# Warm-up products from a constant, a PSUM bank for each sum of the first step, and attention work moved later in a fused attention and SwiGLU kernel

## The chip, the cores and the metric

The kernel runs on one core of one Trainium2 chip. The metric is the device time of one execution in microseconds (us), and lower is better. Every execution has its own time and its own mean granted TensorE clock (1.000 is full speed). All executions below are of the state that the listing calls fast. A verdict of faster or slower needs 2%, which is 6.6 us; a smaller difference is called "same".

The engines are PE (TensorE, products), PEld (its weight loads), DVE (VectorE), ACT (ScalarE), POOL (GpSimd) and SP (the queue that issues transfers).

## The reference

```python
def phi(x):                                   # x: (4, 4, 1088, 32)
    a = np.einsum('rd,bhsd->bhsr', S1, x)     # r = 8
    b = np.einsum('rd,bhsd->bhsr', S2, x)
    return np.einsum('bhsi,bhsj->bhsij', a, b).reshape(*x.shape[:-1], r * r)
q_p, k_p = phi(q), phi(k)
kv  = np.einsum('bhsf,bhsd->bhfd', k_p, v)
z   = np.sum(k_p, axis=2)
num = np.einsum('bhsf,bhfd->bhsd', q_p, kv)
den = np.einsum('bhsf,bhf->bhs', q_p, z)[..., None] + 1e-06
x   = (num / den).transpose(0, 2, 1, 3).reshape(4352, 128)
g   = x @ w_gate                              # 128 x 1536
out = (g / (1 + np.exp(-g))) * (x @ w_val) @ w_out
```

The weights and the sketches S1 and S2 arrive as float64 words. The kernel narrows them to float32 on the chip.

## The kernel before

The tokens are cut into 12 blocks (three per batch, of 384, 384 and 320 tokens) and the hidden layer into 12 chunks of 128. A *unit* is one chunk of one block: a gate product and a value product, a silu on ScalarE, and a product of the two on VectorE that writes `hj`. Each unit has a *down* product with `w_out`, which adds into one bank per block.

```python
free_banks = ["g0", "g1", "g2", "acc"]        # the ring of PSUM banks
turn = [0]
def bank(tag=None):
    if tag is None:
        tag = free_banks[turn[0] % len(free_banks)]
        turn[0] += 1
    return psum.tile([P, TB], FP32, tag=tag, name="bank")

def unit(i, j, late=False):
    g, u = bank(), bank()
    for o, w in ((g, wg), (u, wv)):
        nc.tensor.matmul(o[:, 0:n], w[:, j, :], xT[:, t0 : t0 + n], start=True, stop=True)
    nc.scalar.activation(sg[:, 0:n], g[:, 0:n], AF.Silu)
    ...
    nc.vector.tensor_tensor(out=hj[:, 0:n], in0=sg[:, 0:n], in1=u[:, 0:n], op=ALU.mult)

def down():
    ...
    if j == 0:
        acc[i] = bank("g0" if i == 1 else "acc")
    nc.tensor.matmul(acc[i][:, 0:n], wo[:, j, :], hidden.pop((i, j))[:, 0:n], ...)
```

At the start nothing can be hidden. The program runs products that nobody reads (`keep_warm`), then batch 0's first attention step as a serial chain. For one batch, `kv` and `z` are summed, turned by a product with the identity (`turn_kv`, result copied to `kvz`), and multiplied with the query features (`totals`). Then VectorE divides (`dT` is the transposed denominator, `xT` the result).

```python
keep_warm(98, 32)
...
srep = bank()                                 # sketches turned; takes g0
...
keep_warm(3)                                  # lands in the next bank of the ring
```

After six early units the first three blocks run in a list of 30 units, z = 0 to 29. Batch 1's attention is a generator that advances one piece at each z in `groups`. A `catch_up` is the product `hj` of an early unit, put off and made by GpSimd.

```python
groups = (11, 13, 15, 17, 21, 24, 27)
for z, (i, j) in enumerate(seq):
    if z == 17:
        free_banks.pop()                      # "acc" leaves the ring: 4 banks, then 3
    unit(i, j)
    ...                                       # weight conversions of this z
    if z in (2, 4, 8, 14, 20, 22):
        catch_up()
    if z >= 17:
        ...; down()
    if z in groups:
        next(att)
while todo:                                   # the rounds
    for _ in range(4):
        if todo:
            down()
    next(att, None)
```

Batches 1 to 3 follow in a steady loop, in which the next batch's attention is threaded between units.

Of the kernel before, what the change touches and what calls it, by code (L numbers as in the profile page):

```python
# [17 lines left out]
def kernel(  # L18
# [70 lines left out]
    def wide(tag):  # L89
        return psum.tile([P, 2, TB], FP32, tag=tag, name=tag)  # L90
# [80 lines left out]
    warm = const.tile([P, TB], mybir.dt.bfloat16, name="warm")  # L171
    nc.vector.memset(warm[:], 1.0)
# [16 lines left out]
    def keep_warm(n, w=TB):  # L189


        ps = bank(free_banks[turn[0] % len(free_banks)])
        for _ in range(n):
            nc.tensor.matmul(
                ps[0:32, 0:w], warm[:, 0:32], warm[:, 0:w], start=True, stop=True
            )
# [128 lines left out]
    def turn_kv(kvz, kvs, t, kzp):  # L325

        for half in range(2):
            nc.tensor.matmul(  # L328
                kzp[F * half : F * half + F, P * t : P * t + P], kvs[:, t, :], ident[:],
                start=True, stop=True,  # L330
            )
        nc.scalar.copy(kvz[:, t, :], kzp[:, P * t : P * t + P])
# [58 lines left out]
    def totals(n, phq, kvz, tag):  # L391

        w = 32 * n
        nd = wide(tag)[:].rearrange("p g (t w) -> p g t w", t=2)
        for t in (1, 0):
            for h in range(H):
                for half in range(2):
                    r = slice(F * half, F * half + F)
                    nc.tensor.matmul(  # L399
                        nd[32 * h : 32 * h + 32, half, t, 0:w],  # L400
                        kvz[r, t, 32 * h : 32 * h + 32],
                        phq[r, h, 0:w],
                        start=True,
                        stop=True,
                    )
        return nd

    def divide(b, x0, n, nd):


        w = 32 * n
        t0 = S * b + 64 * x0
        dT = apool.tile([P, 2 * XS, 32], FP32, tag="dT", name="dT", bufs=2)
        rc = apool.tile([P, 2 * XS], FP32, tag="rc", name="rc", bufs=2)
        rd = apool.tile([P, 2 * XS, 32], FP32, tag="rd", name="rd", bufs=2)
        nc.vector.transpose(  # L416
            out=dT[:, 0 : 2 * n, :].rearrange("p (a x) t -> p a x t", a=2),
            in_=nd[:, :, 1, 0:w].rearrange("p a (x t) -> p a x t", t=32),
        )
        nc.vector.tensor_scalar_add(rc[:, 0 : 2 * n], dT[:, 0 : 2 * n, 0], 1e-6)  # L420
        nc.vector.reciprocal(rc[:, 0 : 2 * n], rc[:, 0 : 2 * n])
        nc.vector.transpose(
            out=rd[:, 0 : 2 * n, :], in_=rc[:, 0 : 2 * n].unsqueeze(2).to_broadcast([P, 2 * n, 32])
        )
        nc.vector.tensor_tensor(
            out=xT[:, t0 : t0 + 2 * w].rearrange("p (x a t) -> p a x t", a=2, t=32),
            in0=nd[:, :, 0, 0:w].rearrange("p a (x t) -> p a x t", t=32),
            in1=rd[:, 0 : 2 * n, :].rearrange("p (a x) t -> p a x t", a=2),
            op=ALU.mult,
        )  # L430
# [12 lines left out]
    def attention(b):  # L443
# [26 lines left out]
        kzp = wide("b")  # L470
        for t in range(2):
            turn_kv(kvz, kvs, t, kzp[:, t, :])
        yield
        tags = "ab"
        for i, (x0, n) in enumerate(steps):
            phq = query_features(n, query_products(x0, n, tags))
            if i + 1 < len(steps):
                turn_q(*steps[i + 1])
            elif b + 1 < B:
                load_q(b + 1)  # L480
            yield
            divide(b, x0, n, totals(n, phq, kvz, tags[0]))
            tags = tags[::-1]
            yield
# [72 lines left out]
    keep_warm(98, 32)  # L557
# [10 lines left out]
    srep = bank()  # L568
# [8 lines left out]
    keep_warm(3)  # L577
# [11 lines left out]
    prods = [key_products(bank(), *c, aside=(c[1] == NC)) for c in fpieces]  # L589
    phk = apool.tile([P, NC, H, R, R], FP32, tag="phk", name="phk")  # L590
    kvp = wide("b")
    kz, kv = kvp[:, 0, 0 : H * F], kvp[:, 1, 0:F]
# [4 lines left out]
    pss = query_products(*steps[0], ("a", (None, None)))  # L597
    qbs = [query_copy(n, *ps) for ps in pss]
# [7 lines left out]
    kvs = apool.tile([P, 2, F], FP32, tag="kvs", name="kvs")  # L606
    kvz = apool.tile([P, 2, P], FP32, tag="kvz", name="kvz", bufs=2)
    nc.scalar.copy(zq[:], kz)
    part("wg", 0)
    part("wv", 0)  # L610
# [3 lines left out]
    zp = bank()  # L614
# [5 lines left out]
    key_values(kv, phk, *fpieces[2])  # L620
    turn_q(*steps[1])
    nc.vector.tensor_copy(kvs[:, 1, :], zp[:, 0:F])
    turn_kv(kvz, kvs, 1, bank())
    nc.vector.tensor_copy(kvs[:, 0, :], kv)
    turn_kv(kvz, kvs, 0, bank())
    part("wg", 0)
    part("wv", 0)
    nd = totals(n, phq, kvz, "a")
    pss = query_products(*steps[1], ("b", (None, None)))
    qbs = [query_copy(steps[1][1], *ps) for ps in pss]  # L630
    keep_warm(3)
# [12 lines left out]
    nd = totals(steps[1][1], phq, kvz, "b")  # L644
# [16 lines left out]
    nd = totals(steps[2][1], phq, kvz, "a")  # L661
# [18 lines left out]
    groups = (11, 13, 15, 17, 21, 24, 27)  # L680
    for z, (i, j) in enumerate(seq):
# [5 lines left out]
        if z in (2, 4, 8, 14, 20, 22):  # L687
            catch_up()
# [11 lines left out]
    while todo:  # L700
        for _ in range(4):
            if todo:
                down()
        next(att, None)
# [48 lines left out]
```

## Time and profile before

| | before |
|---|---|
| time given for it, 3 executions | 328.15, 328.80 and 328.87 us |
| execution that the profile shows | 327.24 us, mean clock 1.000 |
| span, first to last instruction | 325.5 us |
| first ordinary unit (z = 0) | 29.46 us |
| first unit with a down product (z = 17) | 56.23 us |
| first unit of batch 1 | 103.09 us |
| last end on TensorE | 321.03 us |

The bottom four rows are starts and one end on TensorE in the profile. TensorE is the bound in all stretches after the start (busy 96% of the span, and 86% of the chain that ended last), so the distance between two such marks is what a stretch costs.

### The profile page before, as it was taken

How to read it: one execution, taken by the hardware profiler on the slowest of the kernel's cores; microseconds unless marked ns; L12 is line 12 of the kernel's file. 1: busy time of each engine (PE TensorE's matmuls, PEld its weight loads, DVE VectorE, ACT ScalarE, POOL GpSimd, SP SyncE). 2: the span in 40 equal slices, each digit the busy share in tenths (PEclk: the TensorE clock that was granted, in tenths of full speed). 3: DMA queues.
4: the chain of work that ended last, by engine and by line, in shares of the span. 5: the costliest groups of instructions: out<-in, count | busy, mean ns of one | idle time of the engine just before them, and what ended most of it. 6: DMA issues, size and time to landing. Idle time of an engine off the chain costs nothing.

```text
span 325.5 us, 5806 instructions
## 1 busy us (share of the span) xinstructions
PE 312.0 (96%) x2402; PEld 187.8 (58%) x2402; DVE 159.0 (49%) x330; ACT 99.1 (30%) x230; POOL 38.5 (12%) x53
## 2 busy tenths in 40 slices
PE   6979997999999999999999999999999999999994
PEld 5435544655556665555666656555567655555672
DVE  4796889542455632444552552345544322322321
ACT  3457554423112222323232222223232222222220
POOL 2222442740000060000000050000000000000000
PEclk9999999999999999999999999999999999999999
DMA  7443473020113202100030100000010000100101
GB/s 209 135 159 99 129 224 117 0 71 0 27 20 85 81 0 71 24 2 0 15 81 2 22 2 0 13 13 2 0 26 0 13 7 2 25 0 0 24 2 20
DMA packets 25018, 14.01 MB, mean 43 GB/s; under 512 B 18848, under 2 KB 23072, under 8 KB 24992
## 3 DMA queue, kind: packets, MB, share of 16 engines
q1 hardware_dynamic: 24304, 13.56, 16.1%
q8 instruction: 19, 0.31, 0.4%
q10 hardware_dynamic: 688, 0.08, 0.2%
q14 instruction: 7, 0.06, 0.1%
HBM read 11.41 MB, written 2.23 MB: 42 GB/s over the span
## 4 chain that ended last, share of the span: by engine, by line
PE 86%; DVE 7%; DMA 2%; issue 2%; ACT 2%; POOL 0%; SPq 0%; DVEq 0%
PE bank L500 49%; PE bank L528 27%; PE a L399 2%; PE a L351 2%; DMA kld<-in_k_dram 1%; PE b L351 1%; PE a L305 1%; DVE hj L514 1%; DMA raw<-in_moe_w_out_dram 1%; DVE man L228 1%; DVE man L217 1%; PE b L328 1%; PE b L399 1%; DVE exp L224 1%; DVE exp L216 1%
## 5 line engine op out<-in xcount | busy, mean ns | idle before, releaser
L514 DVE TENSOR_TENSOR hj<-sg,bank 128x384 f32<-128x384 f32 (+1 forms) x138 | 72.6, 528 | 124.4 <-PE bank L500 120.5
L506 ACT ACTIVATE sg<-bank 128x384 f32<-128x384 f32 (+1 forms) x144 | 67.6, 472 | 167.0 <-PE bank L500 167.0
L500 PE MATMUL bank<-xT,wg 128*128 128x384 f32 (+1 forms) x288 | 114.3, 478 | 4.1 <-DVE hj L514 1.9
L500 PE MATMUL bank<-xT,wv 128*128 128x384 f32 (+1 forms) x288 | 112.1, 471 | 0.3 <-DVE hj L514 0.2
L528 PE MATMUL bank<-hj,wo 128*128 128x384 f32 (+1 forms) x288 | 108.6, 470 | 0.0
L500 PEld LDWEIGHTS bank<-xT,wv 128*128 128x128 f32 x288 | 54.0, 190 | 35.7 <-DVE hj L514 4.4
L500 PEld LDWEIGHTS bank<-xT,wg 128*128 128x128 f32 x288 | 52.3, 190 | 38.5 <-issue 5.7
L528 PEld LDWEIGHTS bank<-hj,wo 128*128 128x128 f32 x288 | 54.2, 190 | 33.0 <-issue 1.4
L436 POOL TENSOR_TENSOR zs<-phk 128x1024 f32<-128x1024 f32 x3 | 7.1, 2358 | 114.5 <-PE bank L500 113.0
L379 DVE TENSOR_TENSOR phq<-a,qb 128x384 f32<-128x384 f32 (+1 forms) x11 | 5.8, 530 | 8.2 <-ACT qb L365 8.2
L365 ACT COPY qb<-a 128x384 f32<-128x384 f32 (+1 forms) x11 | 5.1, 461 | 15.1 <-PE b L351 7.6
L416 DVE STREAM_TRANSPOSE dT<-a 128x384 f32<-128x384 f32 (+1 forms) x8 | 4.4, 550 | 10.7 <-PE a L399 10.7
L228 DVE SCALAR_TENSOR_TENSOR man<-raw,man 128x384 f32<-128x384 uint32 (+2 forms) x14 | 9.3, 666 | 0.0
L351 PE MATMUL b<-qT,sq 32*64 32x192 f32 (+1 forms) x176 | 9.2, 324 | 0.0
L351 PE MATMUL a<-qT,sq 32*64 32x192 f32 (+1 forms) x176 | 9.2, 324 | 0.0
L221 ACT ACTIVATE exp<-exp,rebias 128x384 int32<-128x384 int32 (+3 forms) x15 | 8.2, 547 | 3.0 <-DVE exp L216 2.4
L365 ACT COPY qb<-b 128x384 f32<-128x384 f32 (+1 forms) x11 | 5.1, 464 | 12.8 <-PE b L351 8.0
L224 DVE SCALAR_TENSOR_TENSOR exp<-raw,exp 128x384 int32<-128x384 int32 (+2 forms) x14 | 8.0, 569 | 0.9 <-ACT exp L221 0.9
L379 DVE TENSOR_TENSOR phq<-b,qb 128x384 f32<-128x384 f32 (+1 forms) x11 | 5.8, 526 | 4.5 <-ACT qb L365 4.5
L351 PEld LDWEIGHTS a<-qT,sq 32*64 32x64 f32 x176 | 5.5, 131 | 3.9 <-issue 3.4
L544 DVE STREAM_TRANSPOSE o<-bank 128x384 f32<-128x384 f32 (+1 forms) x12 | 6.7, 558 | 1.7 <-PE bank L528 1.3
L232 POOL TENSOR_TENSOR wg<-man,exp 128x384 f32<-128x384 f32 (+2 forms) x5 | 4.6, 926 | 23.9 <-DVE man L228 23.9
(88 smaller groups left out, 163.7 us busy)
## 6 DMA issues: line engine op xcount, KB each, us to landing
kld<-in_k_dram SPq DMA_DIRECT2D x4, 544.0 KB, 4.3
vld<-in_v_dram SPq DMA_DIRECT2D x12, 144.0 KB, 5.0
qld<-in_q_dram SPq DMA_DIRECT2D x3, 544.0 KB, 4.0
raw<-in_moe_w_out_dram SPq DMA_DIRECT2D x4, 384.0 KB, 3.2
out_dram<-o SPq DMA_DIRECT2D x32, 48.0 KB, 1.8
raw<-in_moe_w_gate_dram SPq DMA_DIRECT2D x3, 384.0 KB, 3.2
raw<-in_moe_w_val_dram SPq DMA_DIRECT2D x3, 384.0 KB, 3.5
out_dram<-o SPq DMA_DIRECT2D x14, 40.0 KB, 1.7
```

The costliest lines, as they stand in the source:

```text
L221: nc.scalar.activation(e[:], e[:], AF.Relu, bias=rebias[: shape[0], :], scale=8.0)
L224: nc.vector.scalar_tensor_tensor(out=e[:], in0=hi, scalar=-(1 << 31), in1=e[:], op0=ALU.bitwise_and, op1=ALU.bitwise_or,)
L228: nc.vector.scalar_tensor_tensor(out=f, in0=lo, scalar=2.0**-52, in1=f, op0=ALU.mult, op1=ALU.add)
L351: nc.tensor.matmul(parts[g][F * half : F * half + F, t, 0:w], sq[r, t, :, :].rearrange("p i j -> p (i j)"), qT[r, x0 : x0 + n, half, :], s ...
L365: nc.scalar.copy(qb[:, :, 0:w], both[:, :, 1, 0:w])
L379: nc.vector.tensor_tensor(out=phq[:, 2 * pr : 2 * pr + 2, 0:w], in0=both[:, :, 0, 0:w], in1=qb[:, :, 0:w], op=ALU.mult,)
L399: nc.tensor.matmul(nd[32 * h : 32 * h + 32, half, t, 0:w], kvz[r, t, 32 * h : 32 * h + 32], phq[r, h, 0:w], start=True, stop=True,)
L436: add = lambda o, a, b: nc.gpsimd.tensor_tensor(out=o, in0=a, in1=b, op=ALU.add)
L500: nc.tensor.matmul(o[:, 0:n], w[:, j, :], xT[:, t0 : t0 + n], start=True, stop=True)
L506: nc.scalar.activation(sg[:, 0:n], g[:, 0:n], AF.Silu)
L514: nc.vector.tensor_tensor(out=hj[:, 0:n], in0=sg[:, 0:n], in1=u[:, 0:n], op=ALU.mult)
L528: nc.tensor.matmul(acc[i][:, 0:n], wo[:, j, :], hidden.pop((i, j))[:, 0:n], start=(j == 0), stop=(j == NCH - 1),)
```

## The change

Its intent has four parts. The unread products at the start take their operand from a constant of the program, with no memset before them, and there are more of them. Each sum, turned matrix and total of the first step gets its own PSUM bank, so that none waits for a neighbour's reader. In later batches the two turned halves go to one bank with one copy. Batch 1's attention pieces start six units later, and a round has three down products and not four. The diff, cut to its core:

```diff
-    warm = const.tile([P, TB], mybir.dt.bfloat16, name="warm")
-    nc.vector.memset(warm[:], 1.0)
+    warm = nc.const_aps.tensor(1.0, [P, TB], mybir.dt.bfloat16)
...
-    keep_warm(98, 32)
+    keep_warm(125, 32)
...
-    srep = bank()
+    srep = bank("g0")
...
-    keep_warm(3)
+    keep_warm(7)
...
-    kvp = wide("b")
-    kz, kv = kvp[:, 0, 0 : H * F], kvp[:, 1, 0:F]
+    kz, kv = bank("g0")[:, 0 : H * F], wide("b")[:, 0, 0:F]
...
-    nd = totals(n, phq, kvz, "a")
+    nd = totals(n, phq, kvz, ([bank(t) for t in ("g2", "acc")], side_by_side("a")[0]))
...
-    keep_warm(3)
+    turn[0] = 2
+    keep_warm(3, ps=wide("a")[:, 0, :])
...
     # attention(b), later batches
-        kzp = wide("b")
+        kzp = wide("b")[:, 0, 0 : 2 * P].rearrange("p (t n) -> p t n", t=2)
         for t in range(2):
-            turn_kv(kvz, kvs, t, kzp[:, t, :])
+            turn_kv(kvs[:, t, :], kzp[:, t, :])
+        nc.scalar.copy(kvz[:], kzp)
...
-    groups = (11, 13, 15, 17, 21, 24, 27)
+    groups = (17, 19, 21, 23, 27, 29)
...
-        if z in (2, 4, 8, 14, 20, 22):
+        if z in (4, 10, 16, 24, 25, 26):
...
-        for _ in range(4):
+        for _ in range(3):
```

Left out are the moved copies and conversions of the first step, and the changed signatures.

More of the change, by code (lines that the diff above doesn't have):

```diff
@@ L187, with keep_warm @@
         nc.gpsimd.memset(sel[32 * a : 32 * a + 1, :], 1.0)
-    def keep_warm(n, w=TB):
-        ps = bank(free_banks[turn[0] % len(free_banks)])
+    def keep_warm(n, w=TB, ps=None):
+        if ps is None:
+            ps = bank(free_banks[turn[0] % len(free_banks)])
         for _ in range(n):
@@ L323, in unit_sums, with turn_kv @@
             )
-    def turn_kv(kvz, kvs, t, kzp):
+    def turn_kv(kvs, kzp):
         for half in range(2):
             nc.tensor.matmul(
-                kzp[F * half : F * half + F, P * t : P * t + P], kvs[:, t, :], ident[:],
-                start=True, stop=True,
+                kzp[F * half : F * half + F, 0:P], kvs, ident[:], start=True, stop=True
             )
-        nc.scalar.copy(kvz[:, t, :], kzp[:, P * t : P * t + P])
     def query_products(x0, n, tags):
@@ L389, in query_features, with halves, totals @@
         return phq
-    def totals(n, phq, kvz, tag):
+    def halves(x):
+        return x if isinstance(x, list) else [x[:, 0, :], x[:, 1, :]]
+    def totals(n, phq, kvz, nd):
         w = 32 * n
-        nd = wide(tag)[:].rearrange("p g (t w) -> p g t w", t=2)
         for t in (1, 0):
@@ L399, in totals @@
                     nc.tensor.matmul(
-                        nd[32 * h : 32 * h + 32, half, t, 0:w],
-                        kvz[r, t, 32 * h : 32 * h + 32],
+                        halves(nd[t])[half][32 * h : 32 * h + 32, 0:w],
+                        kvz[t][r, 32 * h : 32 * h + 32],
                         phq[r, h, 0:w],
@@ L406, in totals, with side_by_side @@
         return nd
+    def side_by_side(tag):
+        both = wide(tag)[:].rearrange("p g (t w) -> p g t w", t=2)
+        return both[:, :, 0, :], both[:, :, 1, :]
     def divide(b, x0, n, nd):
@@ L417, in divide @@
             out=dT[:, 0 : 2 * n, :].rearrange("p (a x) t -> p a x t", a=2),
-            in_=nd[:, :, 1, 0:w].rearrange("p a (x t) -> p a x t", t=32),
+            in_=nd[1][:, :, 0:w].rearrange("p a (x t) -> p a x t", t=32),
         )
@@ L424, in divide @@
         )
-        nc.vector.tensor_tensor(
-            out=xT[:, t0 : t0 + 2 * w].rearrange("p (x a t) -> p a x t", a=2, t=32),
-            in0=nd[:, :, 0, 0:w].rearrange("p a (x t) -> p a x t", t=32),
-            in1=rd[:, 0 : 2 * n, :].rearrange("p (a x) t -> p a x t", a=2),
-            op=ALU.mult,
-        )
+        xs = xT[:, t0 : t0 + 2 * w].rearrange("p (x a t) -> p a x t", a=2, t=32)
+        rs = rd[:, 0 : 2 * n, :].rearrange("p (a x) t -> p a x t", a=2)
+        if isinstance(nd[0], list):
+            todo = [(xs[:, a], nd[0][a][:, 0:w], rs[:, a], "p (x t) -> p x t") for a in (0, 1)]
+        else:
+            todo = [(xs, nd[0][:, :, 0:w], rs, "p a (x t) -> p a x t")]
+        for x, num, r, pat in todo:
+            nc.vector.tensor_tensor(
+                out=x, in0=num.rearrange(pat, t=32), in1=r, op=ALU.mult
+            )
     def feature_sums(phk):
@@ L469, in attention @@
         kvz = apool.tile([P, 2, P], FP32, tag="kvz", name="kvz", bufs=2)
-        kzp = wide("b")
+        kzp = wide("b")[:, 0, 0 : 2 * P].rearrange("p (t n) -> p t n", t=2)
         for t in range(2):
-            turn_kv(kvz, kvs, t, kzp[:, t, :])
+            turn_kv(kvs[:, t, :], kzp[:, t, :])
+        nc.scalar.copy(kvz[:], kzp)
+        kvz = kvz[:, 0, :], kvz[:, 1, :]
         yield
@@ L481, in attention @@
             yield
-            divide(b, x0, n, totals(n, phq, kvz, tags[0]))
+            divide(b, x0, n, totals(n, phq, kvz, side_by_side(tags[0])))
             tags = tags[::-1]
@@ L588 @@
         turn_k(*c)
-    prods = [key_products(bank(), *c, aside=(c[1] == NC)) for c in fpieces]
+    prods = [
+        key_products(bank(t), *c, aside=(c[1] == NC))
+        for t, c in zip(("g1", "g2", "acc"), fpieces)
+    ]
     phk = apool.tile([P, NC, H, R, R], FP32, tag="phk", name="phk")
-    kvp = wide("b")
-    kz, kv = kvp[:, 0, 0 : H * F], kvp[:, 1, 0:F]
+    kz, kv = bank("g0")[:, 0 : H * F], wide("b")[:, 0, 0:F]
     n = steps[0][1]
@@ L596 @@
     turn_q(*steps[0])
-    pss = query_products(*steps[0], ("a", (None, None)))
-    qbs = [query_copy(n, *ps) for ps in pss]
+    pss = query_products(*steps[0], ("a", ("g1", "acc")))
+    qbs = [query_copy(n, *pss[0])]
     key_features(phk, prods[1], *fpieces[1])
@@ L605 @@
     zq = apool.tile([P, H * F], FP32, tag="zq", name="zq")
-    kvs = apool.tile([P, 2, F], FP32, tag="kvs", name="kvs")
-    kvz = apool.tile([P, 2, P], FP32, tag="kvz", name="kvz", bufs=2)
+    kvs, zs = (apool.tile([P, F], FP32, name=x) for x in ("kvs0", "zs0"))
+    kvz = [apool.tile([P, P], FP32, name=x) for x in ("kvz0", "kvz1")]
     nc.scalar.copy(zq[:], kz)
+    qbs.append(query_copy(n, *pss[1]))
     part("wg", 0)
-    part("wv", 0)
     key_values(kv, phk, *fpieces[0])
@@ L613 @@
     phq = query_features(n, pss, qbs)
-    zp = bank()
+    zp = bank("g2")
     for h in range(H):
@@ L620 @@
     key_values(kv, phk, *fpieces[2])
+    nc.vector.tensor_copy(zs[:], zp[:, 0:F])
+    for t, s, to, tag in ((1, zs, None, "g0"), (0, kvs, kv, "g1")):
+        if to is not None:
+            nc.vector.tensor_copy(s[:], to)
+        ps = bank(tag)
+        turn_kv(s[:], ps)
+        nc.scalar.copy(kvz[t][:], ps[:, 0:P])
+    part("wv", 0)
     turn_q(*steps[1])
-    nc.vector.tensor_copy(kvs[:, 1, :], zp[:, 0:F])
-    turn_kv(kvz, kvs, 1, bank())
-    nc.vector.tensor_copy(kvs[:, 0, :], kv)
-    turn_kv(kvz, kvs, 0, bank())
     part("wg", 0)
     part("wv", 0)
-    nd = totals(n, phq, kvz, "a")
-    pss = query_products(*steps[1], ("b", (None, None)))
+    nd = totals(n, phq, kvz, ([bank(t) for t in ("g2", "acc")], side_by_side("a")[0]))
+    pss = query_products(*steps[1], ("b", ("g0", "g1")))
     qbs = [query_copy(steps[1][1], *ps) for ps in pss]
-    keep_warm(3)
+    turn[0] = 2
+    keep_warm(3, ps=wide("a")[:, 0, :])
     divide(0, *steps[0], nd)
@@ L643 @@
     part("wv", 1)
-    nd = totals(steps[1][1], phq, kvz, "b")
+    nd = totals(steps[1][1], phq, kvz, side_by_side("b"))
     unit(0, 1, late=True)
@@ L660 @@
     unit(1, 2, late=True)
-    nd = totals(steps[2][1], phq, kvz, "a")
+    nd = totals(steps[2][1], phq, kvz, side_by_side("a"))
     divide(0, *steps[2], nd)
```

## The prediction

> **What bounds the kernel now.** I read the page's first part and chain first. The columns of the first line are busy microseconds, share of the span and instructions.
>
> ```profile
> PE 312.0 (96%) x2402; PEld 187.8 (58%) x2402; DVE 159.0 (49%) x330; ACT 99.1 (30%) x230; POOL 38.5 (12%) x53
> PE 86%; DVE 7%; DMA 2%; issue 2%; ACT 2%; POOL 0%; SPq 0%; DVEq 0%
> ```
>
> TensorE sets the end. The first question is whether its own work shrinks, and it does not: the same 432 large products and the same attention products are run, plus 31 unread ones. A gain can only come from time in which TensorE waits, so I looked for that next, in the view of waits of TensorE over the span (us in total, times, longest).
>
> ```profile
> PE bank L500 <- DVE hj L514: 2.2, 2, 1.9
> PE bank L194 <- DVE warm L172: 1.5, 1, 1.5
> PE b L328 <- ACT kvz L332: 1.1, 3, 0.4
> PE bank L500 <- POOL wg L232: 1.1, 1, 1.1
> PE bank L500 <- DVE xT L425: 0.9, 1, 0.9
> PE bank L274 <- DVE kT L257: 0.9, 1, 0.9
> ```
>
> All of it but 0.7 us lies before 80 us. But ends of products are modelled, and a short wait hides under the modelled end of the product before it, so I also read start to start. Two records (one product) of 384 columns take 0.645 us, of 320 columns 0.54 us (68.76 to 69.41, 61.72 to 62.26). From the first ordinary unit (29.46) to the first unit that also has a product of the last layer (56.23) are 26.77 us. It holds 17 units, 11 of 384 and 6 of 320 columns, 11 x 1.29 + 6 x 1.075 = 20.64 us, and 1.14 us of key products. So **4.9 us are lost there**, not 2.2. The largest piece, on TensorE and then on VectorE (start, duration, ...):
>
> ```profile
> 52.74 0.91 PE L500 MATMUL bank<-xT,wg 128*128 128x384 f32 x2
> 53.49 0.81 PE L500 MATMUL bank<-xT,wv 128*128 128x384 f32 x2
> 56.23 0.91 PE L500 MATMUL bank<-xT,wg 128*128 128x384 f32 x2 [1.93 <-DVE hj L514]
> ```
>
> ```profile
> 53.77 0.55 DVE L514 TENSOR_TENSOR hj<-sg,bank 128x384 f32<-128x384 f32 x1
> 54.23 1.48 DVE L294 TENSOR_TENSOR phk<-ka,a 128x1280 f32<-128x1280 f32 x1
> 55.63 0.55 DVE L514 TENSOR_TENSOR hj<-sg,bank 128x384 f32<-128x384 f32 x1
> ```
>
> VectorE is in its queue order: the 1.48 us key features stand before the hidden product that frees the bank. Counting the program's bank turns, that unit is the first after "acc" leaves the ring; 57 turns were taken, 57 mod 3 is g0, and g0 is also the bank of the value product just made (turn 56 mod 4). The next product must therefore wait for the newest hidden product.
>
> The start is a serial chain; these lines carry it, in order of time:
>
> ```profile
> 4.63 0.82 PE L194 MATMUL bank<-warm 128*32 128x512 bf16 x3
> 5.20 0.22 ACT L586 COPY sq<-bank 128x64 f32<-128x64 f32 x1
> 5.60 1.50 DVE L257 STREAM_TRANSPOSE kT<-kld 128x384 f32<-128x384 f32 x3 [0.55 <-DMA kld<-in_k_dram]
> 6.33 1.37 PE L274 MATMUL bank<-s,kT 128*32 128x64 f32 x72 [0.88 <-DVE kT L257]
> ...
> 11.42 0.37 ACT L608 COPY zq<-b 128x256 f32<-128x256 f32 x1 [0.69 <-PE b L317]
> 11.84 0.88 PE L305 MATMUL b<-phk,vld 128*32 128x64 f32 x48 [0.46 <-ACT zq L608]
> ...
> 15.05 0.58 DVE L416 STREAM_TRANSPOSE dT<-a 128x384 f32<-128x384 f32 x1 [0.44 <-PE a L399]
> ```
>
> From dT the chain runs on VectorE to xT (17.31), through two weight conversions and the second step's features to GpSimd's weight product and the second unit at 21.09. From there TensorE is packed until 34.5.
>
> [...] the three 512-column products took 0.82 us with 0.39 for the last, (0.82 - 0.39)/2 = 0.215 us each. It shows a granted clock of 1.00 in every slice, so I see no cold time for more products to win. [...] The 0.46 us above is a wait between two different banks of one two-bank tile, so the data do not need it. [...] Conversions that take 0.55 us alone took 1.35 while GpSimd worked (37.71 and 46.22).
>
> **The change, part by part.**
>
> *Unread products.* The first need no VectorE memset, so they should start near 0.9 us (other engines' first instructions are at 0.81 to 0.99) and not 1.53. The 98 took 2.79 us: (2.79 - 0.19)/97 = 26.8 ns apart. 125 take 3.5 us and end near 4.4; before, 4.32. So the start is early for nothing and what follows is about 0.1 us late. The seven products are worse. `srep` is now asked for by name, the turn stays at zero, and the seven are put into the same bank g0. In the built order their first waits for VectorE and ScalarE, the readers of srep; before, the three had another bank and no wait. ScalarE ends at 5.42, now 5.5; 7 x 0.215 = 1.5 us; key products start near 7.1 instead of 6.33. **+0.75 us.**
>
> *Separate banks for kz and kv.* Key values no longer wait for zq (11.40 to 11.84, 0.44 us). But the two 192-column query copies (0.55 us) are now behind zq on ScalarE, the features that read them (0.61) end near 13.4 in the shifted time, and the copy of the totals comes after them on VectorE. The turned matrix starts near 13.63 against 13.18: 0.3 of the 0.75 are recovered.
>
> *Turned matrix and totals.* The denominators' half of the totals has its own bank, so dT may start when that half is done (14.56 of 15.03): worth 0.45 us if VectorE is free. It is not. The built order puts the query transposition (0.57) and four conversions before dT. The second pair of conversions waits for two ScalarE instructions (0.7) that now follow both kvz copies. By hand, ScalarE ends those at 15.25, the last conversion ends at 15.55, and dT starts there against 15.05. The numerator product as two halves costs 0.61 for 0.56. Second unit: **+0.55 us**, at about 21.6.
>
> *Attention groups later* (first group from unit 11 to 17, key features to 21 and 23). In the crowded stretch VectorE loses 0.77 + 0.65 of key transposition and 1.40 of features, and one of four GpSimd catch-ups moves out, with perhaps 0.8 us of contention. Its work from 31.60 to 56.1 was 24.5 less 2.0 idle, 22.5 us; it falls to about 19 against 20.64 of TensorE. The turn counter is set to 2, so 48 turns precede the same point and 48 mod 3 is g0, which was freed long before. The 2.2 us gap should go and some of the 2.7 us of small ones. I leave 1.7 of 4.9: **-3.2 us**. The 1.14 us of key products only move.
>
> *One kvz copy.* Before, the second turned half waited for the first copy: 72.72 to 73.90, 1.18 us for some 0.75 of work. Three batches: **-1.3 us**.
>
> *Three and not four products per round.* After totals, xT is ready 2.4 us later (87.9 to 90.27). Three 320-column products and one half of the query products give 1.61 + 0.33 = 1.94, so one step should wait near 0.5. **+0.5 us.**
>
> Sum: 0.55 - 3.2 - 1.3 + 0.5 = -3.45; 328.8 - 3.4 = **325.4 us**.
>
> **The rivals.** *VectorE or the output weights stay the bound.* Conversions are unchanged, and stalls of 2.1 us came before any attention work. One load of output weights, released by a conversion at 44.83, landed only at 47.86. Then only the big gap goes, -1.7 less: 327.1. Against it: VectorE had 92% of the stretch once the attention is out, by the count above. *The start.* If seven products did not delay the key products, the start would gain 0.2 and the time be 324.7; if VectorE's order costs more, as when each shifted conversion collides with GpSimd, +1.2 and 326.1. *The moved work stalls later.* After unit 17 only three banks turn; yet before, 1.22 us of features passed at 58.37 with no wait, and a unit with its down product takes 1.94 us of TensorE for 0.55 of VectorE. If it stalls all the same, 326.5. *Everything lost is regained*: 323.7.
>
> **Range and chances.** The middle may gain 1.5 to 4.4, the start lose 1.2 or gain 0.2; the kvz term is the surest. That gives 323.2 to 327.8. Two per cent is 6.6 us, more than all waits named; 322.2 is hardly reached, and 335.4 needs a mechanism I do not see, as a throttled clock.
>
> **What would show it.** Key products near 7.1, key values right behind the unit sums, dT near 15.5, second unit near 21.6. From the first ordinary unit to the first with a down product about 22.3 us, without the 1.9 us wait. No wait of the turned matrix for kvz. Some 0.3 to 0.5 us before the last query products at the end of the first batch. I am wrong if the key products start where they did, if the stretch still loses over 3 us, or if new waits stand after the seventeenth unit.

The three 512-column products and the clock of 1.00 are from before's trace.

## The result

| | before | after |
|---|---|---|
| timed side by side, 4 executions each, median (lowest to highest) | 328.84 (328.15 to 329.41) | 324.37 (324.22 to 324.81) |
| ratio of fast runs, 95% interval | | 0.9867 (0.9846 to 0.9889) |
| profiled execution: time, clock, span | 327.24, 1.000, 325.5 | 324.50, 0.999, 322.8 |

A ratio here is the mean time of one kernel's fast runs over that of the other's of the same rounds, so it is not quite the ratio of the medians. The time lies in the predicted range, 1.0 us below the number.

Two figures do not fit together. The timed medians differ by 4.5 us and the two profiled spans by 2.7. The page of after, its busy line and its chain:

```profile
PE 312.2 (97%) x2433; PEld 189.8 (59%) x2433; DVE 156.5 (48%) x330; ACT 98.7 (31%) x227; POOL 37.6 (12%) x53
PE 89%; DVE 5%; ACT 2%; issue 1%; DMA 1%; POOL 0%; DVEq 0%
```

TensorE's work is the same, and its share of the chain rose by three points, two of them taken from VectorE. In the waits of TensorE in after (us in total, times, longest), nothing over 1.1 us remains:

```profile
PE bank L510 <- POOL wg L232: 1.1, 1, 1.1
...
PE bank L317 <- DVE phk L294: 0.8, 1, 0.8
PE bank L194 <- ACT sq L596: 0.8, 1, 0.8
...
PE bank L510 <- DVE hj L524: 0.3, 1, 0.3
```

The 1.9 us wait for `hj` is 0.3 now, and the waits for `kvz` are gone. The wait of the unread products (L194) for the readers of `srep` is new. Starts on TensorE give the account by stretch:

| stretch on TensorE | before | after | difference |
|---|---|---|---|
| start to z = 0 | 29.46 | 29.61 | +0.15 |
| z = 0 to z = 18, key products counted in both | 28.81 | 25.46 + 1.14 moved | -2.21 |
| z = 18 to first unit of batch 1, without the moved ones | 44.82 | 46.49 - 1.14 | +0.53 |
| first unit of batch 1 to the end | 217.94 | 216.77 | -1.17 |
| sum | | | -2.70 |

The start in after, TensorE in order of time (start, duration, group, idle time before it and its releaser):

```profile
5.46 1.47 PE L194 MATMUL bank<-const-bfloat16-1.0 128*32 128x512 bf16 x6 [0.76 <-ACT sq L596]
6.56 0.31 PE L274 MATMUL bank<-s,kT 128*32 128x64 f32 x6
6.77 0.38 PE L194 MATMUL bank<-const-bfloat16-1.0 128*32 128x512 bf16 x1
6.99 1.17 PE L274 MATMUL bank<-s,kT 128*32 128x64 f32 x66
```

The seven wait until 5.46, and all but six of the key products (L274) start at 6.99, not at 6.33 as before. The end of after's serial start, on ScalarE and VectorE:

```profile
14.54 0.30 ACT L222 ACTIVATE man<-man 128x128 f32<-128x128 int32 x1
...
14.68 0.29 DVE L224 SCALAR_TENSOR_TENSOR exp<-raw,exp 128x128 int32<-128x128 int32 x1 [0.84 <-ACT exp L221]
...
15.09 0.57 DVE L420 STREAM_TRANSPOSE dT<-a 128x384 f32<-128x384 f32 x1
```

VectorE does wait for ScalarE's half of a weight conversion before it turns the denominators, as predicted, but it reaches `dT` at 15.09, where before reached it at 15.05.

The critical place of before, now in after:

```profile
52.55 0.81 PE L510 MATMUL bank<-xT,wg 128*128 128x384 f32 x2
53.68 0.91 PE L510 MATMUL bank<-xT,wv 128*128 128x384 f32 x2 [0.33 <-DVE hj L524]
54.43 0.81 PE L538 MATMUL bank<-hj,wo 128*128 128x384 f32 x2
```

Unit 17 starts its gate product without a wait, at 52.55. Its value product waits a little: it starts 1.13 us later where 0.645 would do, 0.48 lost. The turned matrix in batch 1's attention, before and then after:

```profile
72.72 0.44 PE L328 MATMUL b<-ident,kvs 128*64 128x128 f32 x4
73.53 0.44 PE L328 MATMUL b<-ident,kvs 128*64 128x128 f32 x4 [0.36 <-ACT kvz L332]
73.90 0.91 PE L500 MATMUL bank<-xT,wg 128*128 128x384 f32 x2
```

```profile
80.22 0.66 PE L328 MATMUL b<-ident,kvs 128*64 128x128 f32 x8
80.81 2.20 PE L538 MATMUL bank<-hj,wo 128*128 128x384 f32 x6
```

From the turned matrix to the next product took 1.18 us and takes 0.59. The query products in the rounds go the other way. They took 0.94 us in before (from 90.61 to 91.55, and 97.38 to 98.32). In after the ones at 88.88 take 1.25, and the last ones 1.47, of which this is the end:

```profile
95.55 0.77 PE L349 MATMUL b<-qT,sq 32*64 32x160 f32 x16
96.25 1.88 PE L538 MATMUL bank<-hj,wo 128*128 128x320 f32 x6
```

Bank b's half no longer runs beside the other half; it comes after it. That is 0.31 + 0.53 = 0.84 us.

So the traces hold 2.7 us. For the other 1.8, I had to look at executions and not at one trace.

### The profile page after: what moved, and what is told of

Same layout as the page of the kernel before. It is cut to its first block, busy times and chain, and to the rows that moved or that the text cites. A ratio compares the mean times of both kernels' runs of the same rounds, so it can differ in the third digit from the quotient of the medians.

```text
span 322.8 us, 5871 instructions
## 1 busy us (share of the span) xinstructions
PE 312.2 (97%) x2433; PEld 189.8 (59%) x2433; DVE 156.5 (48%) x330; ACT 98.7 (31%) x227; POOL 37.6 (12%) x53
## 4 chain that ended last, share of the span: by engine, by line
PE 89%; DVE 5%; ACT 2%; issue 1%; DMA 1%; POOL 0%; DVEq 0%
PE bank L510 50%; PE bank L538 28%; PE a L349 2%; PE a L399 2%; PE bank L194 2%; PE b L349 1%; ACT exp L221 1%; PE a L305 1%; DVE exp L216 1%; DMA raw<-in_moe_w_out_dram 1%; PE b L399 1%; PE a L274 1%; PE b L328 1%; DVE exp L224 1%; PE bank L317 0%
## 5 line engine op out<-in xcount | busy, mean ns | idle before, releaser
L228 DVE SCALAR_TENSOR_TENSOR man<-raw,man 128x384 f32<-128x384 uint32 (+2 forms) x14 | 6.9, 491 | 0.0
```

What stands on the lines that cost most here:

```text
L228: nc.vector.scalar_tensor_tensor(out=f, in0=lo, scalar=2.0**-52, in1=f, op0=ALU.mult, op1=ALU.add)
```

## The experiments

My theory after the result: one bank turn makes the middle's gain, the one copy gives 1.8 us, the seven products cost 0.7, and before's median holds something that its profile does not. The rivals: VectorE's load in the middle (the moved groups) makes the gain; the products help by warming TensorE; the rest is scatter. Three sets of four kernels ran, each set on one chip, with its own eleven executions of before (medians 328.15, 328.24 and 328.27). Every kernel gave correct results and all verdicts at 2% are "same", so intervals and levels have to decide.

### e1_before_again: before, unchanged

> The kernel before, unchanged, as its own run. Open: its timed runs were 328.15 to 329.41 us, but its profiled execution only 327.24 (span 325.5), while the changed kernel's profile (324.5) lies among its timed runs (324.22 to 324.81). So the two profiles differ by 2.7 us and the times by 4.4. Theory clock: in most executions of the kernel before TensorE runs some microseconds at the half clock near the start, and the profiled one happened not to; then the runs listed here show a mean clock under 1.000 (1.7 us lost would be about 3.4 us at half clock, some 0.990 to 0.995) and a time that falls with it. Rival chance: the profile was one fast execution of a kernel whose time spreads by 2 us for other reasons (transfers landing earlier); then clocks are 0.998 to 1.000 in all runs and the spread is in the first load's landing. Time near 328.8 either way.

Median 326.79 us (326.50 to 328.91), ratio 0.9975 (0.9943 to 1.0008). The same code gave 326.5 and 328.9 in one set. With the executions of before in all three sets there are 39, and they fall into two groups:

| executions of before | count | mean us | mean granted clock of each |
|---|---|---|---|
| lower level (326.50 to 328.24) | 20 | 327.07 | 0.998 to 1.000 |
| upper level (328.14 to 329.51) | 19 | 328.70 | 0.993 to 0.995 |

The split is by clock; one execution at 328.24 with 0.998 would lie in the upper group by its time, and no run says why. The levels are 1.6 us apart, and the mean of all is 327.86. All of the first session's timed executions of before were over 328.1 and its profile was of the lower kind. That the clock falls with the time is as the theory of the expectation had it. The half clock itself was first shown in the trace of e6 (0.50); where in the execution it falls, this run does not show (e6 does). This explains why times and spans disagreed: the profile could not show what half of the executions contain.

### e2_before_products: the unread products of after, alone

```diff
-    warm = const.tile([P, TB], mybir.dt.bfloat16, name="warm")
-    nc.vector.memset(warm[:], 1.0)
+    warm = nc.const_aps.tensor(1.0, [P, TB], mybir.dt.bfloat16)
...
-    keep_warm(98, 32)
+    keep_warm(125, 32)
...
-    keep_warm(3)
+    keep_warm(7, ps=bank("g0"))
```

> The kernel before with only the unread products of the change: from the program constant, 125 and not 98, then 7 and not 3 into the bank that the scale factors are still read from. By my prediction's step: key products start near 7.0 and not 6.33, so the serial start is longer by some 0.6 us and the time 329.4. By the theory clock: [...]the runs sit at the level of the undisturbed profile, 327.2 plus 0.6, so 327.8, and all their clocks are near 1.000.

Median 328.05 us (327.22 to 328.99), ratio 1.0005 (0.9976 to 1.0035). Three executions lie near 327.26 and three near 328.92, so the expected single time of 327.8 was not met, though all clocks are near 1.000. The lower three are 0.2 us above before's lower level. Most key products start at 6.97 (6.33 in before) and the next unit sums at 8.92 (8.30), so the delay of 0.6 us is real. It does not reach the second unit. In before's trace the second group of unit sums took 1.66 us, from 9.72; here it took 1.06, from 10.35, and both end at 11.4. Before's weight loads stopped for 0.50 us there with "issue" as releaser, which means that the profile shows nothing that they waited for. The profiles of e5 and e7, which have before's start, have no such stop, and e1's has one of 0.29. So one profiled start is no measure of a few tenths: the five profiles with before's start (before, e1, e5, e6, e7) reach the second unit at 21.09, 21.58, 20.49, 21.52 and 21.06. (That of e6 ran at half speed up to 10.26, which is told below.)

### e3_after_oldproducts: after, with the unread products of before

```diff
-    warm = nc.const_aps.tensor(1.0, [P, TB], mybir.dt.bfloat16)
+    warm = const.tile([P, TB], mybir.dt.bfloat16, name="warm")
+    nc.vector.memset(warm[:], 1.0)
...
-    keep_warm(125, 32)
+    keep_warm(98, 32)
...
-    keep_warm(7)
+    keep_warm(3, ps=bank("g1"))
```

> The changed kernel with the old unread products (98 after a memset on VectorE, then 3 in a bank that nobody reads). By my prediction: key products back near 6.3, start shorter by up to 0.5 us, time near 323.9. By the theory clock: runs again lose up to 1.7 us to a half clock near the start, so a time of 325 to 326 although the profile, if it falls in a good execution, shows a shorter start.

Median 323.66 us (323.36 to 323.77), ratio 0.9869 (0.9844 to 0.9894). All five executions are on one level, and the 325 to 326 of the theory clock, which looked for a loss near the start, did not come. After's own lower level is 324.36 (seven executions, see e9), so the products cost 0.7 us. First unit 16.86 and second 20.49, for 17.61 and 21.25 in after. In this trace the three 512-column products took 1.46 us for 0.82 in before's, so they were at about half speed, and nothing after them was late for it.

### e4_after_otherbank: after, with the seven products in a bank that nobody reads

```diff
-    keep_warm(7)
+    keep_warm(7, ps=bank("g1"))
```

> The changed kernel with its 125 and 7 unread products, but the 7 in bank g1, which nobody reads, so that they need not wait for the two scalings. They then run from 4.7 to 6.2 and end before the first transposed keys come (about 6.0 to 6.2). My prediction says the wait cost 0.6 us at the key products; if the start's chain carries it to the second unit, the time is 323.8 to 324.0; if VectorE's queue before the first denominators sets that anyway (it waited 0.84 us for a ScalarE result there), the second unit still starts at 21.2 and the time stays 324.4.

Median 324.14 us (323.74 to 324.63), ratio 0.9885 (0.9862 to 0.9908), one level. That is 0.2 below after's lower level, and the mean, 324.14, is 0.7 below that of after's ten executions (324.82, see e9). The wait for the readers of `srep` is gone and the key products start at 6.76. The first key load landed late in this trace (`kT` at 5.78, for 5.40 in after), so its profile does not separate bank and load to a tenth.

### e5_before_ring: before, and one more turn of the ring

```diff
         if z == 17:
             free_banks.pop()
+            turn[0] += 1
```

> The kernel before with one line more: when the fourth bank leaves the ring, the turn is advanced by one, so that the next gate product takes bank g1, which ScalarE freed long ago, and not g0, which the newest hidden product behind the key features has still to free. Nothing else moves. My theory of the middle: the 1.93 us wait goes, the undisturbed level falls from 327.0 to about 325.1. Theory of the second level: of 21 executions of the kernel before with a listed clock, those at 328.2 to 328.9 have a mean clock of 0.993 to 0.995[...]; if the 1.93 us stop of TensorE in the middle is what brings it about, this kernel has no execution with 0.994 and none near 326.8. Rival: the half clock comes from the gaps of the serial start (5.5 to 6.3 us and after); then about half of the executions stay at 0.994 and 1.5 us above the rest.

Median 324.81 us (324.45 to 325.44), ratio 0.9903 (0.9877 to 0.9929). All six clocks are 0.998 to 1.000. From unit 17 on TensorE in e5:

```profile
53.52 0.81 PE L500 MATMUL bank<-xT,wg 128*128 128x384 f32 x2
...
54.81 0.81 PE L528 MATMUL bank<-hj,wo 128*128 128x384 f32 x2
```

The attention groups stand where they stood in before, VectorE has all of its load, and the 1.93 us wait is gone. The mean of the six is 324.85, which is 2.2 us under before's lower level and 3.0 under its mean. With the wait, the upper level went too.

### e6_before_longstall: before, with a longer stop at the same place

```diff
-    groups = (11, 13, 15, 17, 21, 24, 27)
+    groups = (11, 13, 15, 21, 24, 27)
...
         if z in groups:
             next(att)
+        if z == 15:
+            next(att)
```

Both halves of the key features now stand in VectorE's queue before the newest `hj`.

> The kernel before with both halves of the key features put before the newest hidden product, so that the stop of TensorE at the seventeenth unit grows from 1.9 to some 3.1 us. If a long stop in the middle brings a half-clock window, then all or nearly all executions show a mean clock near 0.994 and a time near 327.0 + 1.2 + 1.6 = 329.8, and the profile shows the half clock in the microseconds after the stop. If the half clock comes from the start, the share of 0.994 stays near a half, times lie at 328.2 and 329.8, and the profile shows the middle at full clock.

Median 330.74 us (330.08 to 331.25), ratio 1.0084 (1.0055 to 1.0113), and all six clocks are 0.990 to 0.994. Here the profile caught what before's had missed. TensorE from unit 17 of e6, then busy time per microsecond (PE, PEld, DVE, ACT, POOL, and then the granted clock, the DMA share and GB/s):

```profile
57.81 1.45 PE L500 MATMUL bank<-xT,wg 128*128 128x384 f32 x2 [3.07 <-DVE hj L514]
59.05 1.48 PE L500 MATMUL bank<-xT,wv 128*128 128x384 f32 x2
```

```profile
57.00:58.00 1.00, 0.19 (x1) 0.20 (x2) 1.00 (x3) 0.00 (x0) 0.64 (x1) 1.00 0.00 0
...
59.00:60.00 1.00, 1.00 (x3) 0.64 (x2) 1.00 (x1) 0.49 (x1) 0.92 (x2) 0.50 0.00 0
...
62.00:63.00 1.00, 1.00 (x5) 0.63 (x4) 0.24 (x2) 0.72 (x2) 0.92 (x2) 1.00 0.00 0
```

After the stop the granted clock falls to 0.50. The trace's record of clock changes dates the fall to 58.05 us and the return to 61.46, 3.413 us later, and the products take 1.24 us from start to start for 0.645. Half of 3.4 us is lost, 1.7 us, about the distance of before's two levels; and 1.7 us of 327 lowers a mean clock by 0.005, as the upper level shows.

The median is 0.9 us over the expected 329.8, and why stays open. In the profiled execution (330.50) the start was at half speed: all 72 key products took 2.15 us for 1.37 in before, and the first clock change on record is at 10.26 us for 4.53. But its second unit, at 21.52, lies within the scatter of the starts above. The three executions at 0.990 were not profiled.

The same record suggests a reason why only half of before's executions have it. In before's trace it has two changes: the first entry, at full clock from 4.53 us, called the release here, and a fall after the end (325.38). They are 320.85 us apart, which is 94 times 3.4133. In after's trace (4.40 and 321.84) they are 93 times that apart, and in e6's (10.26, 58.05 and 61.46) 14 times and once. I read this as a grid of that period, which lies differently against each execution; that the clock changes only on it is not shown. The stretch between two lines is called a window below. With the grid extended from the release, the stop can be laid against it:

| profile | stop of TensorE before unit 17 | grid lines there | clock after it |
|---|---|---|---|
| before | 54.30 to 56.23 | 55.73 inside | full |
| e1 | 54.79 to 56.72 | 55.52 inside | full |
| e2 | 54.32 to 56.25 | 55.32 inside | full |
| e7 | 54.28 to 56.22 | 55.77 inside | full |
| e6 | 54.74 to 57.81 | 54.63 and 58.05, stop whole between | half, from 58.05 |

Where a grid line cuts the stop, no single window has more than 1.49 us of it (e7, 55.77 - 54.28), and in these four profiles the clock stays at full speed. A stop of 1.93 us lies whole in one window of 3.41 with a chance of (3.41 - 1.93) / 3.41 = 43%, an estimate that assumes every phase equally likely; 19 of 39 executions of before are on the upper level. The kernel with the stop of 3.07 us had a mean clock of 0.990 to 0.994 in six of six executions, the one with no stop at this place (e5) 0.998 to 1.000 in six of six.

### e7_before_onecopy: before, with the one bank and one copy in later batches

```diff
-        kzp = wide("b")
+        kzp = wide("b")[:, 0, 0 : 2 * P].rearrange("p (t n) -> p t n", t=2)
         for t in range(2):
-            turn_kv(kvz, kvs, t, kzp[:, t, :])
+            ...                               # both halves, no copy
+        nc.scalar.copy(kvz[:], kzp)
```

> The kernel before with only the later batches' turned matrix changed: both halves into one bank and one copy out. I predicted 0.43 us for each of three batches; the two traces suggest 0.59 each. So the undisturbed level should fall from 327.0 to 325.3 to 325.7, and the second level (clock 0.994) should stay as frequent as before, since neither the start nor the long stop is touched.

Median 326.00 us (325.07 to 326.98), ratio 0.9939 (0.9908 to 0.9969). The two levels are still there. The lower three have a mean of 325.23, 1.8 us below before's lower level, and 3 x 0.59 = 1.77 was read from the traces.

### e8_after_oldgroups: after, with the groups, catch-ups and rounds of before

```diff
-    groups = (17, 19, 21, 23, 27, 29)
+    groups = (11, 13, 15, 17, 21, 24, 27)
...
-        if z in (4, 10, 16, 24, 25, 26):
+        if z in (2, 4, 8, 14, 20, 22):
...
-        for _ in range(3):
+        for _ in range(4):
```

> The changed kernel with the attention groups, the catch-ups and the four products per round of before; the banks, the products and the start stay. By my prediction the groups are worth 3.2 us less 0.5 for the rounds. But the ring of banks no longer meets the newest hidden product (turn 48, not 57), so part of the wait stays away: if the ring was the main thing, the time rises by 0.5 to 1.0 only (325.2); if VectorE's load was, by 2 to 3 (327). A half-clock level is to be seen only if a stop near 2 us comes back.

Median 324.16 us (324.10 to 325.94), ratio 0.9899 (0.9868 to 0.9930). The turn counter is still set to 2 here. Putting the whole move back costs nothing. The one wait left at this place is on the first down product:

```profile
56.27 0.88 PE L538 MATMUL bank<-hj,wo 128*128 128x384 f32 x2 [0.73 <-DVE hj L524]
```

Its lower level (four executions, mean 324.14) is 0.2 below that of after. From z = 0 to batch 1 it takes 71.82 us, after takes 71.95 and before 73.63.

### e9_after_again: after, unchanged

> The changed kernel, unchanged. Two runs with its start (the kernel before with its products, and the changed kernel with the old groups) showed two levels 1.7 us apart although the listed clock was 0.999 to 1.000, which the kernels with the old products, or with the seven in an unread bank, did not (0 of 17 executions). I think that with the new products the first release of the clock can come a window later, before any clock event is on record. If so, some of these executions lie near 326.1 at a clock of 0.998 to 1.000, though all four of the first session were at 324.2 to 324.8. If it is the old groups instead, all stay at 324.2 to 324.8.

Median 325.08 us (324.22 to 325.93), ratio 0.9911 (0.9879 to 0.9943). After has two levels as well, but of another kind: before's upper level has a lower mean clock, after's has not. Three executions are at 324.25 and three at 325.91, and all six clocks are 0.998 to 1.000. Over ten executions of after the mean is 324.82: seven at 324.36 and three at 325.91. The profile of e9 fell on the upper level, and its start reads:

```profile
5.52 2.72 PE L194 MATMUL bank<-const-bfloat16-1.0 128*32 128x512 bf16 x6 [0.76 <-ACT sq L596]
...
8.46 2.03 PE L274 MATMUL bank<-s,kT 128*32 128x64 f32 x66
```

The six products took 2.72 us for 1.47, and the 66 key products 2.03 for 1.17. The second unit is at 22.64 for 21.25. The clock row shows full speed here, because it has no entry before the first change on record; that change, the release, is at 10.26 us in e9 and at 4.40 in after's first trace. The length of the products is the evidence.

The grid fits this in part. In after's first trace the window from 0.98 to 4.40 is filled by unread products, and the release comes at its end. In e9 the window from 0.02 to 3.43 begins before the products do (0.85), the next, 3.43 to 6.85, holds the pause from 4.75 to 5.52 in which the seven wait for `srep`'s readers, and only the third is full. The profile of e12, below, has its grid in nearly the same place (3.36 to 6.78) and no pause, and there the release came at 6.78. The products of e12, and then those of e6, whose grid lies as that of e9 (3.43 to 6.85):

```profile
4.68 2.71 PE L194 MATMUL bank<-const-bfloat16-1.0 128*32 128x512 bf16 x7
7.44 1.21 PE L274 MATMUL bank<-s,kT 128*32 128x64 f32 x72
```

```profile
4.66 1.46 PE L194 MATMUL bank<-warm 128*32 128x512 bf16 x3
6.33 2.15 PE L274 MATMUL bank<-s,kT 128*32 128x64 f32 x72 [0.21 <-DVE kT L257]
```

e6 does not fit so simply. It has before's start, its only pause of 0.2 us or more in that window is the one of 0.21, and its release came at 10.26 all the same. So the length of a pause does not decide alone, and what a window must hold for a release stays open. What rests on runs and not on the grid is the effect of the bank: e4 changes nothing else, has no upper level in six executions, and its mean is 0.7 us below that of after. So the bank of the seven products costs more, on average, than the 0.2 us between the lower levels.

Four kernels have this start, in five sets. The upper level at full mean clock came in 0 of 4 (after's first set), 3 of 6 (e9), 2 of 6 (e8), 3 of 6 (e11) and 3 of 6 (e2) executions, 11 of 28. It came in none of the 11 of e3 and e4, after with no pause before its unread products.

### e10_after_noproducts: after, without the 125 and the 7

```diff
-    keep_warm(125, 32)
...
-    keep_warm(7)
```

> The changed kernel without the first 125 and the next 7 unread products. [...]the key products and what follows run at half clock: their records take longer than 0.219 us each, the profile's first full-clock microsecond lies near 8 to 12 us, and the time is 325 to 327, that is 0.5 to 2.5 over the changed kernel. If the products are worth nothing, the start is shorter by the 0.75 us that they cost and the time is 323.7.

Median 324.91 us (323.99 to 325.33), ratio 0.9902 (0.9873 to 0.9930). The key products start at 6.48, earlier, and run at half speed: all 72 take 2.15 us, for 1.21 in e12. The second unit is at 21.09. The mean, 324.78, is that of after's ten, 324.82. On average the 132 products, placed as in after, win nothing; the expected loss of 0.5 to 2.5 us did not come, nor the expected gain of 0.75. That is not so of unread products at large: e3 is the same kernel with before's 98 and 3 in their place, its mean is 323.61, and its slowest execution (323.77) lies below the fastest here (323.99). Those products win 1.2 us, and after's give that back. (The two sets ran on different chips, on which the medians of before were 328.15 and 328.27.)

### e11_after_round4: after, with four down products per round

```diff
-        for _ in range(3):
+        for _ in range(4):
```

> The changed kernel with four and not three down products between the pieces of attention at the end of the first batch. I predicted that three cost 0.5 us; the trace shows query products of 1.25 and 1.47 us for 0.94 before, so 0.84. Expected 323.5, against 324.4, and those two back at 0.94. If the wait is only moved (to the totals), the time stays.

Median 324.50 us (323.53 to 325.20), ratio 0.9896 (0.9862 to 0.9929). The lower level is 323.71, which is 0.65 below after's, and the two groups of query products take 0.94 us again. Three per round cost what the trace said, nearly. Against e8, which differs only in the groups and catch-ups, e11's lower level is 0.43 better: that is what moving the attention is worth when the rounds are left alone.

### e12_best: what the runs spoke for, together

```diff
-            acc[i] = bank("g0" if i == 1 else "acc")
+            acc[i] = bank("g0" if i == 1 else "g2")
...
-    keep_warm(7)
+    keep_warm(7, ps=bank("g1"))
...
+    part("wv", 0)                             # ahead of the turned matrices ...
...
-    part("wv", 0)                             # ... and not behind them
...
-    groups = (17, 19, 21, 23, 27, 29)
+    groups = (11, 13, 15, 17, 21, 24, 27)
...
-            free_banks.pop()
+            free_banks.remove("g2")
...
-        if z in (4, 10, 16, 24, 25, 26):
+        if z in (2, 4, 8, 14, 20, 22):
...
-        for _ in range(3):
+        for _ in range(4):
```

> A version built from what the runs showed: the changed kernel with the groups, catch-ups and four products per round of before; the bank that leaves the ring at the seventeenth unit is g2 and not the one with the newest value product; the seven products in the unread bank g1; the second weight's ScalarE step again ahead of the copies of the turned matrix. From the old-groups run (lower level 324.1) less its 0.73 us wait for that bank, less 0.4 for the products' bank, less up to 0.5 for the ScalarE order: 322.5 to 323.0, and one level only. If the moved groups were needed after all, 324 or more.

Median 322.94 us (322.53 to 323.55), ratio 0.9848 (0.9820 to 0.9876). This beats both kernels: its six executions lie below all ten of after. The profiled execution is the slowest of the six (323.55). Its seven products are half slow (2.71 us, release at 6.78) and its key products come only at 7.44, and still its second unit is at 21.09, as in before: with the conversion moved ahead, VectorE no longer waits for it in front of `dT`. Unit 17 has no wait. Its parts were not run one by one, so how the further 1.4 us below after's lower level divide is open.

## Why the prediction was right or wrong

The predicted 325.4 us was met by 324.37, and more fairly by 324.82, the mean of after's ten executions. The sign, the bound and the sign of every term held. That the number came so near is in part luck. It starts from 328.8, which is before's upper level, and its terms miss in both directions: the groups by 0.6 too much, the one copy by 0.5 too little (below). The first session flatters the change: all its executions of before were on the upper level and all of after on the lower. Lower level against lower level it is 327.07 to 324.36, -2.7 us, as in the traces; mean of all against mean of all it is 327.86 to 324.82, -3.0.

**Unread products, +0.75.** Right in size: e3 gives 0.7 between the lower levels. The named mechanism, the wait for `srep`'s readers, carries 0.2 of it (e4), and in before the same products cost 0.2 (e2); how the rest of e3's 0.7 divides, no run shows. In the pair of profiles it was hidden, because before's start had the 0.50 us stop (e2) and after's first transposition began at 5.40 for 5.60. "I see no cold time for more products to win" came to the right end, as after's win nothing on average (e10) and before's fewer ones are better (e3), but its ground was false. There is cold time at the start of several profiles, with half-speed products up to the release at 10.26 us in e9 and e6 and at 6.78 in e12; the clock row does not show it. What I missed is that putting the seven behind `srep`'s readers goes with a later release in e9's profile (10.26 us, for 6.78 in e12) and with an upper level in 11 of 28 executions, for none of six in e4; e6 shows a late release (10.26) in before's start too. The upper level of after is 1.55 us above its lower one.

**Start as a whole, +0.55.** The profiles say +0.15, which the scatter of single starts makes worthless as a measure. The step that failed is "dT near 15.5". VectorE waited for ScalarE as worked out, but both were 0.4 us earlier than I had them (15.09). I had shifted a chain from before's unit sums at 11.4 by the 0.75 of the key products, and in after these sums end at 11.43 all the same, since they have no 0.50 us stop.

**Groups later, -3.2.** It measured -2.2 net. I wrote two causes, a lighter VectorE and a bank freed long before, and gave them one sum. (26.77 - 20.64 - 1.14 is 4.99, so the 4.9 in it is 5.0.) e5 and e8 part them. The bank turn alone gives 2.2 us with the load unchanged. Moving the groups adds 0.4 (e11 against e8). The "1.7 of 4.9" left was too small: 2.3 stayed before unit 17 and 0.48 came behind it, on the value product, where I had allowed nothing.

**One kvz copy, -1.3.** It measured -1.76 on the traces and -1.8 in e7. The mis-sized term is the work behind the two halves: I had put 0.75 us for it, and it takes 0.59 each time.

**Three per round, +0.5.** It measured 0.84 on the trace and 0.65 in e11. I had one late step in mind and the trace shows two.

The terms as runs gave them (ring, groups, one copy, rounds, unread products) are -2.2, -0.4, -1.8, +0.65 and +0.7, sum -3.05, against -2.7 between the lower levels. The rest of the first step's reordering was not measured alone, and 0.35 is no more than the scatter within a level.

**The missed term.** The prediction read "a granted clock of 1.00 in every slice" from one profile and named a throttled clock only as a reason for slower. As I read the runs, it was in before already: about half of its executions hold 3.4 us at half clock behind the 1.93 us stop. No profile of an upper execution of before was taken, so this rests on the mean clocks, on e5, on e6's trace and on the grid. Removing the stop (e5, mean 324.85) was worth 2.2 us against the lower level and, in the other half of the executions, 1.6 us more. Of the rivals, *VectorE or the output weights stay the bound* (327.1) falls with e5, and *the moved work stalls later* holds for 0.48 us. *The start* named 324.7, nearest to the mean, but for a start that the trace does not show: the key products did come late (6.99).

One thing stays open. None of e2's six executions has a mean clock near 0.994, although its trace has the same stop; at one half each that is a chance of 1 in 64. Three of the six have the longer time at full mean clock that e9 shows with a late start (about 1.7 us), which would move their stop against the grid, so late starts and half clock may exclude each other for some phases. That is argued, not shown.

## What to carry to other kernels

When a ring of buffers changes its length, count which buffer comes next and which reader frees it: one extra turn of the ring was worth more here than rearranging a whole stage. Before explaining a few microseconds between two profiles, list several executions of each with their mean clocks, and ask which level each profile fell on. In e6 a stop of TensorE of 3.07 us, all but 0.34 us of one 3.41 us window, was followed by 3.41 us at a clock of 0.50; in four profiles a stop of 1.93 us, with at most 1.49 us of it in one window, was not. A half-speed start is read from the length of products (2.72 us for 1.47 in e9), not from the clock row (1.000 there); and unread products have to be timed in several executions, since 132 of them won nothing here and 101 won 1.2 us.
